# Memory numerators and denominators in one product, and the whole order made anew, in a two-layer Infini-attention and GEGLU block

## The chip, the cores and the metric

One core of one Trainium2 chip runs the whole program in one launch. The metric is the device time in microseconds of one execution. Three runs of the kernel before stand beside a profile of one execution. The core has TensorE (PE in the profile; its weight loads are PEld), VectorE (DVE), ScalarE (ACT), GpSimd (POOL) and SyncE (SP, which here issues nearly all DMAs).

## The reference

The input x has 2048 tokens of 512 values. The program computes attention, then a feed-forward part, and then both again with the same weights. Cut to what matters:

```python
def _A_ref(x, wq, wk, wv, wo, beta):          # H = 32 heads of Dh = 16, N = 4 segments of L = 512
    ...
    for s in range(N):
        logits = einsum('bhqd,bhkd->bhqk', qs, ks) * scale + mask
        a_dot = einsum('bhqk,bhkd->bhqd', softmax(logits), vs)
        pq = phi(qs)                          # phi(t) = t + 1 for t > 0, exp(t) otherwise
        num = einsum('bhld,bhde->bhle', pq, M)
        den = einsum('bhld,bhd->bhl', pq, z)[..., None] + 1e-06
        o = g * (num / den) + (1.0 - g) * a_dot          # g = sigmoid(beta), one value a head
        pk = phi(ks)
        M = M + einsum('bhld,bhle->bhde', pk, vs)        # a 16 x 16 memory for each head
        z = z + einsum('bhld->bhd', pk)                  # and its normaliser, 16 values
    return o @ wo
def _B_ref(x, w_gate, w_up, w_down):          # 512 -> 1792 -> 512
    return _gelu(x @ w_gate) * (x @ w_up) @ w_down
x = x + _A_ref(_layernorm(x), ...); x = x + _B_ref(_layernorm(x), ...)    # and both lines once more
```

## The kernel before, in words

The work is cut into eight blocks k = 0..7: four segments of 512 tokens in the first layer, then the same four in the second. Block k has an attention part (`Att`) and a feed-forward part (`Ffn`). Everything stays in on-chip memory (SBUF) but the weights' first load and the output. Products go to the eight banks of PSUM, 512 float32 values wide; VectorE or ScalarE reads them out from there.

**Attention of one block.** Four tiles `xn` of normalised tokens are transposed to `xnT`, by DMA (line 754, on SP's queue) or by four TensorE transposes against `ident` (line 545). From `xnT` come q, k and v (`wq_sb`, `wk_sb`, `wv_sb`; 12 products of four accumulated matmuls). The scores are made in rounds: 36 rounds a block, taken two at a time, four matmuls side by side on TensorE's four row groups; each pair of rounds fills two pairs of banks, and ScalarE takes the exponential of each pair into `pt` (line 1864). GpSimd masks `pt` (lines 1813 and 1818), and a flush (`flush_item`) multiplies `pt` with v (`vaug`, `vz`) on the four column groups. VectorE turns, divides and turns back the result (lines 1391 to 1414) into `aT`, which meets `wo_sb`.

**Memory.** From block 1 of a layer on, `mem_items` reads the memory: 16 small products of 8 columns give the denominators (`zcols`, line 1195 and the reciprocal in line 1200 make `rdm`), then for each of four groups of 8 heads four products of 128 columns give the numerators (`mblk`), which VectorE scales to `am` (line 1226); a DMA transposes `am` to `amT`, and VectorE adds it to `aT` (line 1417). `upd_item` brings the memory up to date: `spread` writes `mblk` (line 1286) and `z` writes `zcols` (line 1292).

**Feed-forward.** `wo` products are added to `x_sb`, the row statistics are taken (line 856), `xn` is made (line 920) and transposed, then 14 gates, 14 ups and 4 downs per block (four matmuls each, a down has 14) with the gelu on ScalarE.

**What sets the order.** All engines' instructions are recorded in an order that `order()` settles as the program is built. It keeps a clock for each engine (`Clocks`, `Engine`), with fixed costs, picks the item with the earliest due time among those that its clock calls ready (`pick`, `open_item`), and issues scores when ScalarE's queue runs short (`rounds_now`). Some forty numbers (`POLICY`, and `STAGES` for each stretch of 20 us) weigh these choices. Where the clock finds scores still to come but nothing ready, it issues a fill, a product of `warm` that nobody reads. Products go out `whole` (one matmul of 128 x 128 weights) or in `columns` (four matmuls of 32 columns of weights each), whichever stands next to a flush; scores are `rows`. On the chip the engines then follow this order, waiting on each other's semaphores.

Of the kernel before, what the change touches and what calls it, by code (L numbers as in the profile page):

```python
# [17 lines left out]
P = 128  # L18
D = 512
# [13 lines left out]
SCALE = DH ** -0.5  # L33
EPS_LN = 1e-5
# [31 lines left out]
def table(halved):  # L66
# [17 lines left out]
    if halved:  # L84
# [31 lines left out]
    rs_pool=32.757, f_urge=-233.244, quick=2, paired=8, turn_pe=1, turn_last=0, w_at=29.345, w_gap=2.17,  # L116
    wd_at=78.552, wd_gap=2.776, flush_wait=-13.887, piece_slack=40.254, kb_slack=24.368, mem_slack=-20.134,
    margin=0.5, qk_due=0.962, e_q=49.408, e_k=2.993, exp_slack=-6.401, e_slack=131.01, phi_slack=22.785,
    gelu_slack=-0.789, act_evict=1.671, first_evict=0.248, gate_step=93.832, up_due=-100.529, up_step=84.355,
    down_due=-29.196, down_step=-47.297, upd_due=91.807, kb_act=82.777, vz_slack=55.93, x_dve=2.467, v0_due=-11.641,  # L120
    x1_at=-87.497, x2_at=16.051, x3_at=24.107, x3_load=-378.834, direct=2, gelu_tiles=0, look=3, lag=0.852,
    wv_at=-320.502, xn_pool=19.822, kb_pool=121.576, cut_pool=154.009, at_pool=-238.466, pe_turns=0, gate_due=4.191,
    shun=8.799, col_gap=0.807, hold=5, early=104.615, starve=0.16, near=114.234, cap=13, soon=28.208, columns=0,
    kd_slack=-5.85, zero_slack=-1.031, hold1=-49.923, hold2=2.205, hold3=11.541, hold_step=-162.485, hold_v=23.995,
    park=3)

STAGES = [
    (1, 2, dict(
        rs_pool=0.722, quick=9, kb_slack=2.193, mem_slack=-24.231, e_q=-2.643, gelu_slack=-0.49, gate_step=79.021,
        up_due=-101.483, up_step=41.973, down_step=-58.4, upd_due=91.729, vz_slack=33.291, direct=8, gelu_tiles=2,  # L130
        lag=0.412, at_pool=-237.424, early=83.209, starve=60.426, soon=7.146, park=4)),
    (2, 3, dict(
        rs_pool=2.667, quick=6, turn_pe=0, kb_slack=55.298, mem_slack=-32.756, e_q=-2.851, gelu_slack=-0.49,
        gate_step=78.038, up_due=-98.977, up_step=25.491, down_step=-53.827, upd_due=91.729, vz_slack=14.093,
        x_dve=7.459, direct=6, gelu_tiles=2, look=2.764, lag=0.475, xn_pool=30.206, cut_pool=102.189,
        at_pool=-237.424, gate_due=8.415, starve=1.292, soon=7.146, park=5)),
    (3, 4, dict(
        rs_pool=4.794, turn_pe=12, kb_slack=51.509, mem_slack=58.674, e_q=50.036, e_k=1.445, gelu_slack=1.935,
        gate_step=78.038, up_due=-96.513, up_step=85.14, down_step=-56.495, vz_slack=40.138, x_dve=6.187, direct=6,
        look=2.618, xn_pool=30.206, cut_pool=118.125, at_pool=-208.534, gate_due=14.291, shun=21.0, early=101.394,  # L140
        starve=0.321, soon=7.146, park=2)),
    (4, 5, dict(
        rs_pool=-2.341, quick=0, turn_pe=12, kb_slack=85.554, mem_slack=58.674, qk_due=1.009, e_q=50.137, e_k=1.464,
        gelu_slack=0.429, gate_step=79.294, up_due=-96.513, up_step=84.505, down_step=-72.139, vz_slack=51.333,
        x_dve=6.187, direct=3, gelu_tiles=2, xn_pool=20.238, cut_pool=148.746, at_pool=-208.534, gate_due=8.415,
        shun=21.0, early=101.394, starve=0.453, soon=7.146, park=2)),
    (5, 6, dict(
        rs_pool=36.794, quick=0, turn_pe=12, kb_slack=66.017, mem_slack=58.674, qk_due=1.009, e_q=55.15, e_k=2.984,
        gelu_slack=-0.805, gate_step=79.294, up_due=-96.513, down_step=-70.89, vz_slack=18.865, x_dve=7.455,
        gelu_tiles=2, look=2.835, lag=0.71, xn_pool=20.238, cut_pool=148.746, at_pool=-208.534, gate_due=0.276,  # L150
        shun=21.488, soon=7.146)),
    (6, 7, dict(
        rs_pool=11.417, f_urge=-261.392, quick=0, paired=11, turn_pe=0, flush_wait=0.581, piece_slack=36.524,
        kb_slack=76.591, mem_slack=-10.427, qk_due=-0.609, e_q=97.288, e_k=-5.757, exp_slack=-18.942, e_slack=69.536,
        phi_slack=30.587, gelu_slack=0.965, act_evict=1.166, gate_step=33.55, up_due=-80.509, down_due=-55.61,
        down_step=-81.567, upd_due=143.06, kb_act=60.08, vz_slack=4.039, x_dve=18.331, direct=0, gelu_tiles=2,
        look=2.622, lag=0.754, xn_pool=-3.088, kb_pool=116.679, cut_pool=153.155, at_pool=-189.709, gate_due=0.226,
        shun=85.539, hold=8, early=169.131, starve=0.31, near=101.522, cap=11, soon=0.694, kd_slack=37.99, park=6)),
    (7, 8, dict(
        rs_pool=-52.581, f_urge=-61.761, quick=3, paired=0, turn_pe=13, flush_wait=-3.039, piece_slack=92.516,  # L160
        kb_slack=220.906, mem_slack=57.517, qk_due=-30.647, e_q=-54.782, e_k=89.983, exp_slack=-17.861,
        e_slack=55.594, phi_slack=96.482, gelu_slack=214.751, act_evict=-149.173, gate_step=5.34, up_due=-0.69,
        up_step=3.923, down_due=12.354, down_step=-3.42, upd_due=-3.412, kb_act=75.691, vz_slack=-199.522,
        x_dve=3.843, direct=4, gelu_tiles=6, look=1.342, lag=0.004, xn_pool=-28.912, kb_pool=53.965, cut_pool=27.06,
        at_pool=-56.962, gate_due=-1.429, shun=104.852, hold=14, early=6.432, starve=57.777, near=-2.631, cap=0,
        soon=-55.855, kd_slack=-7.989, park=5)),
    (8, 9, dict(
        rs_pool=-52.581, f_urge=-145.617, quick=3, paired=0, turn_pe=9, flush_wait=-5.724, piece_slack=95.692,
        kb_slack=220.647, mem_slack=59.145, qk_due=-29.873, e_q=-54.782, e_k=89.76, exp_slack=-17.752,
        e_slack=55.641, phi_slack=95.445, gelu_slack=218.63, act_evict=-149.173, gate_step=5.34, up_due=-2.89,  # L170
        up_step=10.443, down_due=12.354, down_step=-3.42, upd_due=-3.412, kb_act=75.691, vz_slack=-188.382,
        x_dve=3.864, direct=5, gelu_tiles=6, lag=0.004, xn_pool=-26.431, kb_pool=53.965, cut_pool=27.06,
        at_pool=-56.962, gate_due=-1.429, shun=104.852, hold=14, early=6.432, starve=57.777, near=-2.631, cap=0,
        soon=-86.977, kd_slack=-7.989, park=5)),
    (9, 10, dict(
        rs_pool=-12.084, f_urge=-80.924, paired=7, turn_pe=0, flush_wait=-10.54, piece_slack=101.497,
        kb_slack=138.651, mem_slack=41.847, qk_due=-0.927, e_q=5.553, e_k=3.345, exp_slack=8.894, e_slack=112.615,
        phi_slack=35.259, gelu_slack=68.681, act_evict=-22.963, gate_step=1.861, up_due=1.655, up_step=-0.829,
        down_due=2.632, down_step=52.765, upd_due=23.459, kb_act=0.175, vz_slack=70.28, x_dve=6.676, direct=3,
        look=3.63, lag=0.192, xn_pool=166.767, kb_pool=117.564, cut_pool=-34.878, at_pool=-118.909, gate_due=-0.418,  # L180
        shun=0.067, hold=0, early=-9.041, starve=0.14, near=123.977, cap=10, soon=-75.197, kd_slack=-0.85, park=4)),
    (10, 11, dict(
        rs_pool=14.701, f_urge=-84.002, quick=4, paired=3, turn_pe=0, flush_wait=1.591, piece_slack=2.503,
        kb_slack=15.492, mem_slack=-87.956, qk_due=-1.255, e_q=-12.885, e_k=30.907, exp_slack=-49.037,
        e_slack=61.889, phi_slack=62.891, gelu_slack=12.108, act_evict=-26.178, gate_step=1.032, up_due=-0.726,
        up_step=0.248, down_due=2.892, down_step=13.594, upd_due=48.393, kb_act=-2.244, vz_slack=6.293,
        x_dve=-53.841, direct=7, gelu_tiles=4, look=0.488, lag=0.594, xn_pool=9.388, kb_pool=94.753, cut_pool=-5.876,
        at_pool=-15.364, gate_due=2.814, shun=1.865, hold=4, early=0.773, starve=0.337, near=15.239, cap=8,
        soon=11.166, kd_slack=-1.019, park=4)),
    (11, 12, dict(  # L190
        rs_pool=18.476, f_urge=-83.81, quick=3, paired=2, turn_pe=2, flush_wait=1.611, piece_slack=1.938,
        kb_slack=15.492, mem_slack=-82.753, qk_due=-1.255, e_q=13.513, e_k=-8.54, exp_slack=-36.188, e_slack=75.196,
        phi_slack=62.891, gelu_slack=10.942, act_evict=-15.505, gate_step=0.996, up_due=-0.689, up_step=0.248,
        down_due=6.859, down_step=13.594, upd_due=46.726, kb_act=4.652, vz_slack=6.293, x_dve=-55.157, direct=6,
# [378 lines left out]
def order(pol, nc, cst, seg, wrk, psp, A_x, A_wq, A_wk, A_wv, A_wo, A_beta, B_x, B_w_gate, B_w_up, B_w_down, out):  # L573
# [185 lines left out]
    class Psum:  # L759
# [6 lines left out]
        def read(self, t):  # L766
            banks[self.bank] = t + 0.05
# [1239 lines left out]
```

## Time and profile before

| what | before |
|---|---|
| three runs | 534.12, 535.46, 538.31 us; median 535.46 |
| span of the profiled execution | 533.3 us; its own device time isn't listed apart, and the three runs lie 0.9 to 5.1 us over its span |
| busy: PE, PEld, DVE, ACT, POOL | 524.7, 275.7, 434.6, 445.8, 252.5 us |
| granted TensorE clock | 1.000 over the whole span |
| fetches of instructions by DMA | 83 of 16 KB on one queue, 21 smaller ones on another |

The span runs from the first instruction to the last. The device time of a run lies around it and is a few microseconds longer. A matmul's row gives a duration with its latency, and matmuls overlap; what TensorE spends on one is read from the distance of two starts.

### The profile page before, as it was taken

What the parts mean: (1) busy time and instruction counts of PE and PEld (TensorE: products, weight loads), DVE (VectorE), ACT (ScalarE), POOL (GpSimd) and SP (SyncE); (2) the same over time, 40 slices, a digit from 0 to 9 for tenths busy, and PEclk for the clock granted to TensorE, in tenths of its full rate; (3) what the DMA queues carried; (4) which work ended last, traced back from release to release, by engine and by line L of the source; (5) the groups of instructions that cost most, each with busy time, mean ns of one, the idle gap of its engine ahead of it and who ended that gap; (6) DMA issues with size and microseconds to landing.
All of it is one profiled execution on the core that took longest, in us unless ns stands there. A gap on an engine that the chain in (4) does not pass through costs nothing.

```text
span 533.3 us, 24180 instructions
## 1 busy us (share of the span) xinstructions
PE 524.7 (98%) x10697; PEld 275.7 (52%) x10697; DVE 434.6 (81%) x836; ACT 445.8 (84%) x598; POOL 252.5 (47%) x320
## 2 busy tenths in 40 slices
PE   9999989999999999999999999999999999999997
PEld 4454455444545455555564454555555456555544
DVE  7899997999997999889987788888976997586342
ACT  6999989888999989899898899799979988952320
POOL 2987472548541966428773366391632254400000
PEclk9999999999999999999999999999999999999999
DMA  8367750333330232101221122410250132102101
GB/s 271 76 120 148 190 158 4 69 39 77 42 69 16 53 56 38 32 12 25 53 41 31 25 32 27 60 33 2 53 102 3 33 51 53 23 2 48 37 2 41
DMA packets 76762, 29.99 MB, mean 56 GB/s; under 512 B 61042, under 2 KB 76658, under 8 KB 76658
## 3 DMA queue, kind: packets, MB, share of 16 engines
q1 hardware_dynamic: 76368, 28.20, 25.8%
q8 instruction: 83, 1.36, 1.0%
q10 hardware_dynamic: 290, 0.26, 0.1%
q14 instruction: 21, 0.17, 0.1%
HBM read 9.70 MB, written 2.10 MB: 22 GB/s over the span
## 4 chain that ended last, share of the span: by engine, by line
PE 75%; DVE 5%; ACT 3%; POOL 1%; issue 1%; DMA 1%; ACTq 0%
PE ps L541 75%; ACT pt L1864 1%; DVE xn L920 1%; DVE st L856 1%; ACT gel_sb L1616 1%; POOL kx L726 1%; DVE x_sb L1463 1%; ACT gel_sb L1519 1%; POOL e L1170 1%; DMA xnT<-xn 1%; ACT gel_sb L779 0%; DVE ab L1407 0%; DVE byq L1391 0%; DVE aT L1414 0%; DVE x_sb L869 0%
## 5 line engine op out<-in xcount | busy, mean ns | idle before, releaser
L1864 ACT ACTIVATE pt<-ps 128x1024 bf16<-128x1024 f32 x288 | 279.0, 1036 | 27.5 <-PE ps L541 18.6
L1813 POOL TENSOR_SCALAR_AFFINE_SELECT pt<-pt 128x256 bf16<-128x256 bf16 (+1 forms) x192 | 112.4, 598 | 176.4 <-ACT pt L1864 173.9
L541 PE MATMUL ps<-xnT,wg_sb 128*32 128x512 bf16 (+3 forms) x1367 | 107.7, 362 | 0.2 <-DMA xnT<-xn 0.2
L541 PE MATMUL ps<-wd_sb,gel_sb 128*32 128x512 bf16 (+2 forms) x1431 | 106.1, 354 | 0.0
L541 PE MATMUL ps<-xnT,wu_sb 128*32 128x512 bf16 (+1 forms) x1252 | 103.5, 379 | 0.2 <-ACT gel_sb L1519 0.2
L1557 DVE TENSOR_TENSOR gel_sb<-gel_sb,ps 128x512 bf16<-128x512 bf16 x112 | 75.2, 684 | 30.2 <-PE ps L541 27.9
L541 PEld LDWEIGHTS <-gel_sb 128*32 128x32 bf16 (+1 forms) x1623 | 53.0, 97 | 41.4 <-issue 2.2
L541 PEld LDWEIGHTS <-wu_sb 128*32 128x32 bf16 (+1 forms) x1252 | 45.6, 97 | 45.4 <-issue 2.1
L541 PEld LDWEIGHTS <-wg_sb 128*32 128x32 bf16 (+1 forms) x1367 | 47.4, 97 | 38.7 <-issue 1.4
L1391 DVE STREAM_TRANSPOSE byq<-ps 128x512 f32<-128x512 f32 x64 | 45.3, 709 | 24.0 <-PE ps L541 23.3
L1170 POOL TENSOR_SCALAR e<-e 128x512 bf16<-128x512 bf16 x32 | 49.5, 1550 | 7.0 <-ACT e L1147 6.4
L1463 DVE TENSOR_TENSOR x_sb<-x_sb,ps 128x512 bf16<-128x512 bf16 (+1 forms) x54 | 34.1, 636 | 17.9 <-PE ps L541 17.8
L1818 POOL TENSOR_SCALAR_AFFINE_SELECT pt<-pt 64x1024 bf16<-64x1024 bf16 x32 | 38.5, 1203 | 20.7 <-ACT pt L1864 17.4
L541 PE MATMUL ps<-xnT,wk_sb 128*32 128x512 bf16 (+2 forms) x330 | 34.8, 377 | 0.7 <-ACT pt L1864 0.7
L541 PE MATMUL ps<-pt,vaug 128*32 128x256 bf16 (+2 forms) x1344 | 35.1, 239 | 0.1
L541 PE MATMUL ps<-xnT,wq_sb 128*32 128x512 bf16 (+2 forms) x339 | 34.0, 377 | 0.0
L1616 ACT ACTIVATE gel_sb<-gel_sb 128x1024 bf16<-128x1024 bf16 (+4 forms) x31 | 33.3, 1157 | 0.0
L541 PE MATMUL ps<-wv_sb,xnT 128*32 128x512 bf16 (+1 forms) x227 | 32.4, 380 | 0.8 <-DVE x_sb L1463 0.4
L541 PE MATMUL ps<-q,kx 32*128 32x64 bf16 (+2 forms) x1120 | 31.6, 217 | 0.6 <-ACT pt L1864 0.3
L541 PEld LDWEIGHTS <-vaug 128*32 128x32 bf16 x1344 | 27.1, 97 | 9.2 <-issue 1.6
L856 DVE BATCH_NORM_STATS2 st<-x_sb 128x6 f32<-128x512 bf16 x46 | 31.3, 680 | 0.4
L541 PEld LDWEIGHTS <-kx 32*128 32x128 bf16 x1120 | 17.0, 92 | 28.2 <-issue 27.4
(127 smaller groups left out, 708.7 us busy)
## 6 DMA issues: line engine op xcount, KB each, us to landing
vz<-vaug SPq DMA_DIRECT2D x14, 136.0 KB, 2.9
wg_sb<-in_B_w_gate_dram SPq DMA_DIRECT2D x8, 224.0 KB, 2.9
wu_sb<-in_B_w_up_dram SPq DMA_DIRECT2D x8, 224.0 KB, 3.9
wd_sb<-in_B_w_down_dram SPq DMA_DIRECT2D x7, 256.0 KB, 5.9
x_sb<-in_A_x_dram SPq DMA_DIRECT2D x3, 512.0 KB, 6.7
out_dram<-x_sb SPq DMA_DIRECT2D x12, 128.0 KB, 1.9
xnT<-xn SPq DMA_TRANSPOSE x56, 2.6
kx<-kf SPq DMA_DIRECT2D x12, 64.0 KB, 3.2
```

What stands on the lines that cost most here:

```text
L541: self.nc.tensor.matmul(*args, **kw)
L726: return lambda: eng.tensor_scalar(out=kx[:, :, C * which:C * which + n], in0=kf[:, :, 0:n], scalar1=masks[:, which:which + 1], scalar2=No ...
L856: nc.vector.bn_stats(out=self.st6[:, 0, :], in_=x_sb[:, self.tt0 + j, :])
L920: eng.tensor_scalar(out=xn[:], in0=x_sb[:, self.tt0 + j, :], scalar1=self.mv[:, j, 1:2] if self.wide else self.mv[:, j, 0:1], scalar2=self ...
L1170: lambda eng: eng.tensor_scalar(out=e[0][:], in0=e[0][:], scalar1=1.0, scalar2=None, op0=ALU.min), summed)
L1391: nc.vector.transpose(out=(self.byq[:, pars[0], :, :].rearrange("p a c -> p (a c)") if h is None else self.byq[:].rearrange("p u a c -> p ...
L1463: ck.dve.post(ck.made(), slack, (0.15 + 0.00104 * (c1 - c0), lambda: nc.vector.tensor_tensor(out=xt, in0=xt, in1=ps()[:, 0:c1 - c0], op=AL ...
L1557: ck.dve.post(ck.made(), NORMAL, (0.683, lambda: nc.vector.tensor_tensor(out=g, in0=g, in1=ps()[:], op=ALU.mult), lambda t: (ps.read(t), e ...
L1616: return (0.205 + 0.427 * (f1 - f0), lambda: nc.scalar.activation(out=g, in_=g, func=ACT.Gelu_apprx_tanh), lambda t: self.gelu_done(t, f0, ...
L1813: nc.gpsimd.affine_select(out=view, in_=view, pattern=[[0, 4], [0, n], [1, C]], compare_op=ALU.is_ge, fill=0.0, base=C, channel_multiplier=-1)
L1818: nc.gpsimd.affine_select(out=view, in_=view, pattern=[[0, 4 * TPS], [1, C]], compare_op=ALU.is_ge, fill=0.0, base=0, channel_multiplier=-1)
L1864: nc.scalar.activation(out=pt_all[:, s0:s0 + 2, 2 * p:2 * p + 2, :].rearrange("p r h c -> p h r c"), in_=ps_all[:, pair[0]:pair[1] + 1, :] ...
```

## The change

- **Memory read.** Denominators become a ninth part of the numerators: `mz` holds for each head 16 columns of M and one of z, so 136 columns a group of 8 heads instead of 128 and 8 apart. Instead of 16 products of 8 columns and then 16 of 128 there are 16 of 136. They come in three items; each fills a pair of neighbouring banks (`Pair`), two items with one and a half groups and one with one. VectorE then does, for each item in one go, the denominators, a reciprocal and the scaling.
- **Memory update.** `spread` writes `mz` in four instructions instead of one.
- **Scores.** Where enough banks are free, the four banks of two rounds are taken by one exponential of 2048 columns instead of two of 1024 (`joined`).
- **Head.** The product for beta uses all 128 rows (`beta_row` is cleared by GpSimd first) and stands one product later. GpSimd clears the two `kx` tiles instead of VectorE, and writes the constant columns of three of four v tiles.
- **End.** The last down product of each block of the second layer is cut 384 + 128 instead of 256 + 256.
- **Planner's clock.** Each fetch of TensorE's instructions now makes a busy stretch on SP's queue: an SP instruction that ends near it ends later, and a DMA transpose that starts near it lands later, and no sooner than 0.45 us after the one before. All numbers of `POLICY` and `STAGES` are new, and with them the order of all engines.

```diff
+MZ = (DH + 1) * 8
 POLICY = dict(
-    rs_pool=32.757, f_urge=-233.244, quick=2, paired=8, turn_pe=1, turn_last=0, w_at=29.345, w_gap=2.17,
+    rs_pool=-104.717, f_urge=-138.301, quick=0, paired=6, turn_pe=0, turn_last=0, w_at=29.345, w_gap=-0.624,
...
     # Engine.serve, for SP
+            for begin, end in self.fetches[-3:]:
+                if -0.15 < begin - t < (0.85 if cost > 1.0 else 0.35):
+                    t = max(t, end + (0.45 if begin > t else 1.07) - cost)
     # Clocks.issue
             self.asked.append(self.pe)
+            begin = self.pe + 1.1
+            self.fetches.append((begin, begin + (1.5 if self.dma > begin else 1.05)))
     # Clocks.landing
-        for a in self.asked[-3:]:
-            if -0.6 < a + 1.1 - t < 1.1:
-                got = max(got, a + 2.3 + (1.5 if a + 1.1 < t + 0.1 else 1.1))
+        for begin, end in self.fetches[-3:]:
+            if -0.5 < begin - t < 1.3:
+                got = max(got, end + (1.55 if begin < t + 0.3 else 1.1))
+        self.turned = got = max(got, self.turned + 0.45)
     # head
-    nc.scalar.dma_start(out=beta_row[:], in_=A_beta.partition_broadcast(1))
+    nc.scalar.dma_start(out=beta_row[0:1, :], in_=A_beta.partition_broadcast(1))
+    for kx in kxs:
+        nc.gpsimd.memset(kx.bitcast(mybir.dt.uint32)[:, :, :, C // 2:3 * C // 2], 0)
-    te.matmul(beta_ps, lhsT=warm[0:1, :], rhs=beta_row[:], start=True, stop=True)
     a0.first_q(ps2, 0, half)
+    te.matmul(beta_ps, lhsT=warm[:], rhs=beta_row[:], start=True, stop=True)
     # mem_items
-                product(dens()[:, j, b, :], self.phiq[:, b, j * P:(j + 1) * P], mem_state[k - 1][1][:, b, :])
-                    product(ps()[:, j * P:(j + 1) * P], self.phiq[:, b, j * P:(j + 1) * P], mem_state[k - 1][0][:, b, :])
+            parts = [((0, 0, None), (1, 4, 0)), ((2, 0, None), (1, 4, 1)), ((3, 0, None),)]
+                ps = Pair()
+                    product(ps()[:, i, MZ * u:MZ * u + MZ], self.phiq[:, b, j * P:(j + 1) * P], mem_state[k - 1][0][:, b, :])
+                    steps = [(0.175, den(whole, 0, 2, 0, 4), None)]
+                    if half:
+                        steps.append((0.157, den(1, 2, 3, 4, 6), None))
+                    steps.append((0.454 if half else 0.354, inverse, None))
+                    if half:
+                        steps.append((0.42, scale(1, 2, 3, 4, 6, 2 * n, 2 * n + 2), None))
+                    steps.append((0.69, scale(whole, 0, 2, 0, 4, 0, TPS), told))
+                    ck.dve.post(ready, NORMAL, *steps)
     # Ffn, second layer
-                downs[-1:] = [down(TPS - 1, 0, D // 2), down(TPS - 1, D // 2, D)]
+                downs[-1:] = [down(TPS - 1, 0, D - P), down(TPS - 1, D - P, D)]
     # score
+        joined = bool(runs) and len(got) - 4 >= pol.join
...
+            def exp_all(b0=pairs[0][0]):
+                nc.scalar.activation(
+                    out=pt_all[:, s0:s0 + 2, :, :].rearrange("p r h c -> p h r c"),
+                    in_=ps_all[:, b0:b0 + 4, :].rearrange("p h (r c) -> p h r c", r=2), func=ACT.Exp, scale=SCALE)
```

**VectorE at the first memory read** (block 1; `gel_sb` are the feed-forward's products, `ab`, `aT` the attention's, `e` and `zk` the keys' phi). Before:

```order
L1195 SCALAR_TENSOR_TENSOR rdm<-ps,tmp_e_135 128x128
L1200 RECIPROCAL rdm<-rdm 128x128
L1557 TENSOR_TENSOR gel_sb<-gel_sb,ps 128x512 x3
L1226 TENSOR_TENSOR am<-ps,rdm 128x512 x2
L1557 TENSOR_TENSOR gel_sb<-gel_sb,ps 128x512 x3
```

Now:

```order
L1227 SCALAR_TENSOR_TENSOR rdm<-ps,tmp_e_138 128x32
L1227 SCALAR_TENSOR_TENSOR rdm<-ps,tmp_e_138 128x16
L1235 RECIPROCAL rdm<-rdm 128x48
L1242 TENSOR_TENSOR am<-ps,rdm 128x256
L1242 TENSOR_TENSOR am<-ps,rdm 128x512
L1227 SCALAR_TENSOR_TENSOR rdm<-ps,tmp_e_138 128x32
```

Before, the feed-forward's multiplications stand between the steps of the memory read; now five instructions stand together for each of the first two items, and the two items follow each other.

**SyncE's queue near the end** (`xnT<-xn` is the transpose for a normalised tile, `amT<-am` that of the memory's part, `out_dram` the output). Before:

```order
L754 DMA_TRANSPOSE amT<-am 128x4x128 x2
L600 DMA out_dram<-x_sb 128x256 x2
L754 DMA_TRANSPOSE amT<-am 128x4x128 x2
L754 DMA_TRANSPOSE xnT<-xn 128x4x128 x4
L600 DMA out_dram<-x_sb 128x512 x3
```

Now:

```order
L752 DMA_TRANSPOSE xnT<-xn 128x4x128 x4
L599 DMA out_dram<-x_sb 128x512
L599 DMA out_dram<-x_sb 128x384
L599 DMA out_dram<-x_sb 128x128
L752 DMA_TRANSPOSE amT<-am 128x4x128 x4
L599 DMA out_dram<-x_sb 128x512 x3
```

The four transposes for the last block's feed-forward are gone from the queue; TensorE makes them (16 transposes of 128 x 128 between the downs of block 6). Over the whole program SP issues 40 instead of 56 transposes of `xn`, and TensorE 96 instead of 32.

More of the change, by code (lines that the diff above doesn't have):

```diff
@@ L152 @@
-    (6, 7, dict(
[L153 to L158, printed above, removed]
@@ L159 @@
-    (7, 8, dict(
[L160 to L166, printed above, removed]
```

544 lines of the change are left out of this document (298 added, 246 removed).

## The prediction

> **What bounds the kernel now.** I read the page's busy times and the chain that ended last, then busy times by stretch, then TensorE's own order of time at the holes.
>
> ```profile
> span 533.3 us, 24180 instructions
> PE 524.7 (98%) x10697; PEld 275.7 (52%) x10697; DVE 434.6 (81%) x836; ACT 445.8 (84%) x598; POOL 252.5 (47%) x320
> PE 75%; DVE 5%; ACT 3%; POOL 1%; issue 1%; DMA 1%; ACTq 0%
> ```
>
> TensorE is busy for 98% of the span and holds three quarters of the chain. So only two things move the time: how much TensorE has to do, and how long it stands still. The stretches (columns: width, then busy time of PE, PEld, DVE, ACT, POOL, granted clock, DMA share and rate) show where it stands.
>
> ```profile
> 0.00:9.00 9.00, 7.77 (x43) 3.79 (x44) 5.82 (x19) 5.32 (x13) 2.16 (x14) 1.00 0.80 241
> 20.00:40.00 20.00, 19.68 (x386) 10.09 (x388) 17.66 (x38) 19.89 (x31) 17.34 (x23) 1.00 0.54 107
> 40.00:60.00 20.00, 19.28 (x486) 10.26 (x475) 17.84 (x34) 19.92 (x25) 13.39 (x19) 1.00 0.75 165
> 60.00:80.00 20.00, 18.28 (x361) 9.70 (x359) 18.56 (x39) 17.42 (x30) 12.04 (x13) 1.00 0.59 165
> 80.00:100.00 20.00, 19.78 (x364) 10.04 (x366) 15.37 (x27) 19.50 (x24) 3.84 (x7) 1.00 0.12 29
> 120.00:140.00 20.00, 19.30 (x460) 9.66 (x453) 19.10 (x40) 18.06 (x27) 14.83 (x18) 1.00 0.38 65
> 140.00:160.00 20.00, 19.55 (x336) 9.88 (x338) 19.29 (x35) 19.18 (x26) 8.91 (x12) 1.00 0.32 61
> 180.00:300.00 120.00, 119.77 (x2401) 64.11 (x2400) 106.10 (x201) 108.24 (x140) 69.69 (x83) 1.00 0.20 38
> ```
>
> Of the 8.6 us of idle time (533.3 - 524.7), 1.2 lie in the first 9 us, and 4.1 between 20 and 160: 0.32, 0.72, 1.72, 0.22, 0.70 and 0.45. The 120 us after 180 lose 0.23. ScalarE or VectorE is full in the losing stretches (19.9 of 20 at 20 to 60, 19.1 and 19.3 at 120 to 160). The granted clock, third from the end of each row, is 1.00 everywhere, so throttling plays no part.
>
> ```profile
> 70.15 0.55 PE L541 MATMUL ps<-warm 128*128 128x128 bf16 x7
> ...
> 71.12 0.20 PE L541 MATMUL ps<-q,kx 32*128 32x64 bf16 x1
> 71.58 0.29 PE L541 MATMUL ps<-q,kx 32*128 32x64 bf16 x7 [0.26 <-ACT pt L1864]
> ...
> 74.56 0.29 PE L541 MATMUL ps<-q,kf 16*128 16x64 bf16 x7
> 76.09 0.36 PE L541 MATMUL ps<-q,kf 16*128 16x192 bf16 x5 [1.24 <-issue]
> q8 instruction: 83, 1.36, 1.0%
> ```
>
> Seven fills in a row at 70.15 mark a place with nothing to do. The largest hole, before 76.09, is put down to no engine, in a place with short matmuls and many instructions; I take it for a late fetch of instructions (queue q8, 83 of them). Note what idle leaves out: from 71.12 to 71.58 pass 0.46 us, while matmuls side by side start within a few ns, yet only 0.26 count as idle, because the latency of the one before covers the rest. So a hole costs about 0.17 to 0.2 more than it shows. With some twenty holes (my estimate), the 4.1 us are about 8.
>
> **The change, part by part.** First, what a product costs. The distance between starts, not the duration, is TensorE's price.
>
> ```profile
> 97.18 2.76 PE L541 MATMUL ps<-xnT,wu_sb 128*128 128x512 bf16 x12
> 99.87 0.41 PE L541 MATMUL ps<-q,kx 32*128 32x64 bf16 x20
> 100.21 0.40 PE L541 MATMUL ps<-mblk,phiq 128*128 128x128 bf16 x4
> 100.44 1.03 PE L541 MATMUL ps<-xnT,wu_sb 128*128 128x512 bf16 x4
> 101.31 0.39 PE L541 MATMUL ps<-mblk,phiq 128*128 128x128 bf16 x4
> ...
> 387.80 1.91 PE L541 MATMUL ps<-wd_sb,gel_sb 128*32 128x512 bf16 x32
> 389.64 0.40 PE L541 MATMUL ps<-q,kf 16*128 16x256 bf16 x12
> ```
>
> Four products of 512 columns take 101.31 - 100.44 = 0.87, 0.217 each; four of 128 take 0.23, 0.057 each. From 97.18 to 99.87, twelve of 512 (2.60) leave 0.09 for the change from whole array to row groups. In column groups eight products (32 matmuls) and such a change take 1.84: 8 x 0.217 + 0.10. So a product costs the same in either form, and a change of form 0.1.
>
> ```profile
> L541 PE MATMUL ps<-zcols,phiq x192: 166/166/179, 89.8 to 439.3; 128*32 128x8 bf16 x128, 128*128 128x8 bf16 x64
> L541 PE MATMUL ps<-zcols,phiq x64: 166/174/178, 89.8 to 90.3; 128*32 128x8 bf16 x64
> L541 PE MATMUL ps<-mblk,phiq 128*128 128x128 bf16 x67 | 5.9, 219 | 0.2 <-ACT pt L1864 0.2
> L541 PE MATMUL ps<-mblk,phiq 128*32 128x128 bf16 x116 | 3.0, 219 | 0.0
> L545 PE MATMUL ps<-ident,xn 128*128 128x128 bf16 x32 | 2.9, 220 | 0.1
> L541 PE MATMUL ps<-warm 128*128 128x128 bf16 x11 | 1.1, 218 | 0.0
> L541 PE MATMUL ps<-warm 128*32 128x128 bf16 x8 | 0.5, 219 | 0.0
> ```
>
> - **Memory read: -2.4.** Six reads have 96 denominators (64 whole, 128 / 4 in columns) and 96 numerators. At 89.8 sixteen denominators take 0.5, 0.03 each: 2.9 go, and with them 96 x 0.057 = 5.5. In their place come 96 of 136 columns, 0.057 x 136 / 128 = 0.061 each: 5.9. The sum is -2.5 by these rows; I take -2.4.
> - **Transposes: +3.6.** TensorE makes 96 instead of 32: 64 x 0.057. Their cover was the DMA, which charged TensorE nothing. The Trainium skill, "VectorE: DVE Perf Modes", section "The three transpose paths", gives 390 ns for one on TensorE and 1309 by DMA, and by that, as an estimate, 64 would cost 25 us and the sum would be 21 higher. The row of 32 speaks against it as a price of TensorE's time: 2.9 us in all, at most 0.09 each.
> - **Fills: -0.7.** In the new order one of 13 (11 and 8 / 4) is left: 12 x 0.057.
> - **Changes of form: +1.2.** Counted over all TensorE rows of both orders there are 292 before and 304 now: 12 x 0.1. Also, fewer products are in columns, so TensorE has 18,384 rows instead of 21,396, and the 83 fetches become about 71.
> - **Head and end: -0.3.** Below nothing for the end: the last addition is 0.42 for 256 columns, now 128, so between 0 and 0.42 goes; I take 0.13 by proportion. The one-row product for beta caused two changes of form on the way in and out, about 0.17. GpSimd's clearing falls in its idle time at the start, and frees VectorE in 9 to 20.
>
> ```profile
> 530.41 0.42 DVE L1463 TENSOR_TENSOR x_sb<-x_sb,ps 128x256 bf16<-128x256 bf16 x1 [1.11 <-PE ps L541]
> L1195 DVE SCALAR_TENSOR_TENSOR rdm<-ps,tmp_e 128x128 f32<-128x128 f32 x6 | 1.7, 278 | 0.0
> L1200 DVE RECIPROCAL rdm<-rdm 128x128 f32<-128x128 f32 x6 | 5.7, 953 | 0.2
> L1401 DVE RECIPROCAL r<-byq 128x32 f32<-128x32 f32 x32 | 11.3, 354 | 1.1
> L1226 DVE TENSOR_TENSOR am<-ps,rdm 128x512 bf16<-128x512 f32 x24 | 15.9, 678 | 1.0 <-PE ps L541 1.0
> ```
>
> - **VectorE: +7, off the path.** A read took 0.28 + 0.95 + 4 x 0.68 = 3.95. Now a full item has two short sums (about 0.2 each), a reciprocal of 48 (0.354 + 16 x 0.6 / 96 = 0.45), a scaling of 256 (0.42 by the addition above) and one of 512: 1.95; the last item 1.23. Together 5.1, so 1.2 more a read, 7 in all, on an engine that is 81% busy. Its cover is the feed-forward's products; without it each read would show 1.2.
> - **The holes: -4.0, the choice on which the sum hangs.** The bounds are 8 (all go) and, below nothing, 8 of new ones. For a gain: the fills tell where TensorE had nothing ready, and 12 of 13 go; the 1.72 at 60 to 80 lie there, with hidden time some 2.5; the thinner instruction stream makes a late fetch rarer; exponentials of all four banks and VectorE's freed start ease 20 to 60. Against all of it: what waits for ScalarE at 20 to 60 stays, and the new order has its own tight places. I take half.
>
> **The sum:** -2.4 + 3.6 - 0.7 + 1.2 - 0.3 = +1.4, and -4.0 for the holes: -2.6. The span goes from 533.3 to 530.7. The median of the runs, 535.46, is 2.2 over the span, which the change doesn't touch, so 532.9.
>
> **The rivals.** *Holes only move* (chance 0.24): the work of TensorE is what is left, +1.4: 536.9. For it: the end has become tight. Before, the last gates had room:
>
> ```profile
> 481.77 12.29 PE L541 MATMUL ps<-wd_sb,gel_sb 128*32 128x512 bf16 x280
> 485.94 5.91 SPq L754 DMA_TRANSPOSE xnT<-xn  x4
> 493.89 2.33 PE L541 MATMUL ps<-xnT,wg_sb 128*32 128x512 bf16 x40
> ```
>
> From the end of the `wo` products (481.77) to the first gate pass 12.1 us of downs, and the transposes have landed or nearly by 491.9, 2 us early. In the new order 14 products each of 512, 384 and 128 columns and 16 transposes stand there (3.0 + 2.3 + 0.8 + 0.9 = 7.0 us), while the additions, statistics and normalisation alone ran to about 486.9, 5.1 us; a late step on VectorE would show at once.
>
> *All holes go* (0.17): 8 instead of 4: 528.9. Against it: ScalarE's 19.9 of 20.
>
> *Memory reads starve the scores* (0.11), the side on which the change is slower. Each of 18 items holds two neighbouring banks until VectorE has done all its steps, up to 1.95 instead of 0.68 for one bank: 18 x 1.27 = 23 us more of holding. If VectorE comes late, a pair of rounds finds no two free pairs, ScalarE runs dry, and TensorE has nothing to follow. It decides where VectorE is over 95% (the stretches from 120 to 160); if half of the 23 reach TensorE, 11 on top of 532.9: about 544. Against it: most reads lie after 180, where VectorE has 12% free.
>
> *A transpose costs TensorE 0.39*, the mechanism to which the page's figure belongs: by the busy 0.09 a transpose it is all but shut out (0.01, about 554).
>
> **How the numbers follow.** The forecast has 0.47. The range of 528.5 to 539 takes in it, the two rivals on either side of it and the scatter of the runs (534.1 to 538.3), and leaves out the starved scores. One per cent, 5.4 us, is about what a measurement of this kernel tells from no change: faster means under 530.1, slower over 540.8. Faster has the 0.17 of all holes gone and 0.03 of the forecast's edge, 0.20; slower 0.12; same 0.68.
>
> **What would show it.** In the profile after: TensorE's idle time in 20 to 160 near 2 instead of 4.1, no gap of over 1 us at issue near 75, fetches near 71, `mz` products 0.06 apart, transposes 0.057 apart. Wrong would be: waits of the exponentials for VectorE around `am`, gaps before the last block's gates or `wo` products, or idle time after 180 above 1 us.

## The result and the profile after

| | before | now |
|---|---|---|
| median of four runs each | 535.33 us (534.12 to 538.31) | 557.30 us (555.29 to 557.96) |
| ratio | | 1.040, 95% interval 1.037 to 1.043 |
| profiled execution: span, TensorE idle | 533.3, 8.6 us | 553.4, 30.9 us |

The prediction was 532.9, with 528.5 to 539.0. The change costs 22 us by the medians and 20.1 by the two profiled spans, and the profile shows most of it as idle time of TensorE. The page's head and its chain:

```profile
span 553.4 us, 21067 instructions
...
PE 522.5 (94%) x9116; PEld 265.5 (48%) x9191; DVE 442.6 (80%) x892; ACT 444.0 (80%) x576; POOL 259.1 (47%) x341
...
q8 instruction: 72, 1.18, 0.9%
...
PE 64%; DVE 12%; ACT 10%; DMA 5%; issue 5%; POOL 3%; SPq 0%; DVEq 0%; ACTq 0%; POOLq 0%
```

By these rows TensorE's busy time has gone down by 2 and its idle time up by 22, and its share of the chain from 75% to 64%. Some 6 us of the idle time are not real: 9116 matmuls stand beside 9191 weight loads, so 75 records are missing. In the three runs further below that keep TensorE's order and have all records it is busy for 529 to 531 us, so the idle time has grown by about 16. The stretches, for the same times as before:

```profile
20.00:40.00 20.00, 18.59 (x396) 9.20 (x397) 19.02 (x39) 19.35 (x28) 16.57 (x23) 1.00 0.82 145
...
180.00:300.00 120.00, 113.09 (x2086) 56.98 (x2094) 98.39 (x196) 97.61 (x118) 58.37 (x72) 1.00 0.16 29
300.00:420.00 120.00, 113.14 (x2113) 58.88 (x2125) 94.24 (x193) 100.40 (x136) 57.98 (x75) 1.00 0.12 25
```

The last of these rows before:

```profile
300.00:420.00 120.00, 119.90 (x2641) 63.45 (x2640) 99.67 (x188) 109.43 (x143) 56.62 (x70) 1.00 0.24 41
```

Before, the 120 us after 180 lost 0.23 and the next 120 us 0.10; now each loses 6.9, of which 1.4 and 1.3 are missing records. On average no engine is full there (DVE 98 and 94 of 120, ACT 98 and 100), and the clock is 1.00, so too much work on another engine does not explain the idle time. The waits say for what TensorE stood still (columns: total, times, longest):

```profile
PE ps L539 <- DMA xnT<-xn: 6.4, 8, 1.5
PE ps L539 <- issue: 6.2, 39, 0.2
PE ps L539 <- POOL pt L1865: 5.1, 5, 1.5
PE ps L539 <- ACT pt L1917: 2.9, 9, 1.0
PE ps L539 <- DVE gel_sb L1600: 1.9, 6, 0.6
```

Before, there was none for POOL or `gel_sb` of VectorE, and these two rows were:

```profile
PE ps L541 <- ACT pt L1864: 1.5, 5, 0.4
PE ps L541 <- DMA xnT<-xn: 0.2, 1, 0.2
```

The 39 gaps of 0.2 at "issue" are the missing records and not waits: in the three runs with the same order and all records this row is gone. The timeline at one of the five POOL waits shows the pattern:

```profile
358.07 2.04 ACT L1917 ACTIVATE pt<-ps 128x1024 bf16<-128x1024 f32 x2
...
360.17 2.43 POOL L1865 TENSOR_SCALAR_AFFINE_SELECT pt<-pt 64x1024 bf16<-64x1024 bf16 x2 [1.99 <-ACT pt L1917]
...
360.49 0.63 PE L539 MATMUL ps<-pt,vaug 128*32 128x256 bf16 x24
...
362.65 0.30 PE L539 MATMUL ps<-pt,vz 128*32 128x64 bf16 x16 [1.53 <-POOL pt L1865]
```

The flush starts at 360.49, though the last mask that it needs ends at 362.60; TensorE issues its first 24 matmuls and then stands still with the rest at the head of its queue. GpSimd is not late: it started as soon as the exponentials were done. **The flush was put too early in the order.** Two lines of the program, unchanged by the diff, can do that:

```python
for ck.back in (pol.lag, 0.0):       # a flush is ready if each mask's end + 0.1 + ck.back <= ck.pe
t3 = ck.landing(t2) + margin         # when a DMA transpose counts as landed
```

`lag` and `margin` are safety margins in us. In before `lag` is 0.004 to 1.414 and `margin` 0.5 in all 27 stretches of 20 us. In the new set `lag` is -7.9 to -56.6 in 21 of them, and `margin` -0.5 to -66.6 in all. In the other six, up to 60 us and from 100 to 160, `lag` is 7.7 to 37.9, and none of the five mask waits lies there: they come between 199 and 451 us. Below zero, an input counts as there before its end; far below zero, as soon as its end is merely known. The order's clock does not charge the wait, so it sees neither a hole nor the need for a fill.

### The profile page after: what moved, and what is told of

It is laid out like the page before. It is cut to its first block, busy times and chain, and to the rows that moved or that the text cites. A ratio compares the mean times of both kernels' runs of the same rounds, so it can differ in the third digit from the quotient of the medians.

```text
span 553.4 us, 21067 instructions
## 1 busy us (share of the span) xinstructions
PE 522.5 (94%) x9116; PEld 265.5 (48%) x9191; DVE 442.6 (80%) x892; ACT 444.0 (80%) x576; POOL 259.1 (47%) x341
## 4 chain that ended last, share of the span: by engine, by line
PE 64%; DVE 12%; ACT 10%; DMA 5%; issue 5%; POOL 3%; SPq 0%; DVEq 0%; ACTq 0%; POOLq 0%
PE ps L539 63%; ACT pt L1917 7%; DMA xnT<-xn 5%; DVE gel_sb L1600 2%; POOL pt L1865 1%; DVE x_sb L1506 1%; DVE byq L1434 1%; DVE st L861 1%; DVE xn L925 1%; PE ps L543 1%; ACT gel_sb L1562 1%; ACT gel_sb L1659 1%; DVE ab L1450 1%; DVE pt L1870 1%; DVE aT L1457 1%
## 5 line engine op out<-in xcount | busy, mean ns | idle before, releaser
L1917 ACT ACTIVATE pt<-ps 128x1024 bf16<-128x1024 f32 x264 | 252.7, 1038 | 34.6 <-PE ps L539 30.4
L539 PE MATMUL ps<-xnT,wg_sb 128*32 128x512 bf16 (+1 forms) x745 | 105.5, 380 | 4.8 <-DMA xnT<-xn 1.4
L539 PE MATMUL ps<-wd_sb,gel_sb 128*32 128x512 bf16 (+4 forms) x1177 | 102.0, 368 | 3.3 <-issue 1.7
L539 PEld LDWEIGHTS <-gel_sb 128*32 128x32 bf16 (+1 forms) x1383 | 50.5, 97 | 46.6 <-DVE gel_sb L1600 2.0
L539 PEld LDWEIGHTS <-wg_sb 128*32 128x32 bf16 (+1 forms) x766 | 42.5, 97 | 47.9 <-issue 3.7
L1175 POOL TENSOR_SCALAR e<-e 128x512 bf16<-128x512 bf16 x34 | 54.2, 1605 | 13.3 <-ACT e L1152 11.4
L1506 DVE TENSOR_TENSOR x_sb<-x_sb,ps 128x512 bf16<-128x512 bf16 (+2 forms) x58 | 36.6, 641 | 19.2 <-PE ps L539 18.4
L1865 POOL TENSOR_SCALAR_AFFINE_SELECT pt<-pt 64x1024 bf16<-64x1024 bf16 x24 | 28.5, 1189 | 28.9 <-ACT pt L1917 26.7
L861 DVE BATCH_NORM_STATS2 st<-x_sb 128x6 f32<-128x512 bf16 x50 | 33.8, 676 | 0.2
L539 PE MATMUL ps<-wo_sb,aT 128*32 128x512 bf16 (+1 forms) x283 | 31.2, 380 | 1.0 <-ACT pt L1917 0.5
```

The source lines that it names most:

```text
L539: self.nc.tensor.matmul(*args, **kw)
L861: nc.vector.bn_stats(out=self.st6[:, 0, :], in_=x_sb[:, self.tt0 + j, :])
L1175: lambda eng: eng.tensor_scalar(out=e[0][:], in0=e[0][:], scalar1=1.0, scalar2=None, op0=ALU.min), summed)
L1506: ck.dve.post(ck.made(), slack, (0.15 + 0.00104 * (c1 - c0), lambda: nc.vector.tensor_tensor(out=xt, in0=xt, in1=ps()[:, 0:c1 - c0], op=AL ...
L1865: nc.gpsimd.affine_select(out=view, in_=view, pattern=[[0, 4 * TPS], [1, C]], compare_op=ALU.is_ge, fill=0.0, base=0, channel_multiplier=-1)
L1917: nc.scalar.activation(out=pt_all[:, s0:s0 + 2, 2 * p:2 * p + 2, :].rearrange("p r h c -> p h r c"), in_=ps_all[:, pair[0]:pair[1] + 1, :] ...
```

## Experiments

**Theories.** A: these two numbers put products ahead of their inputs. B: the new parts (memory read in pairs of banks, joined exponentials, more TensorE transposes) make the waits. C: any order made anew misses the chip, since the old one fits it.

All results side by side. The first seven experiments after "now" are one run each, the others medians of 4 to 12. Idle is the span less TensorE's busy time. Fills are products of `warm` 128 wide (whole ones, and columns by four). "DMA" and "masks" are TensorE's waits for transposes by DMA and for `pt` by GpSimd. Five rows have idle time that is 5 to 7 us too high for missing records: now, `lag` -30, `lag` alone held up, new last down, and half masks on VectorE.

| kernel | time | idle | DMA | masks | fills |
|---|---|---|---|---|---|
| before | 535.3 | 8.6 | 0.2 | 0 | 13 |
| now | 557.3 | 30.9 | 6.4 | 5.1 | 1 |
| old code, `margin` -5 | 551.4 | 20.2 | 7.9 | 0 | 17 |
| old code, `lag` -30 | 588.6 | 44.5 | 5.2 | 10.0 | 111 |
| new code, `lag` and `margin` held up | 568.3 | 23.5 | 0 | 0.2 | 108 |
| new code, `lag` alone held up | 579.7 | 35.3 | 3.7 | 0 | 131 |
| old code, all new numbers | 603.6 | 46.7 | 4.9 | 13.0 | 104 |
| new code, all old numbers | 576.5 | 32.2 | 11.5 | 0.6 | 143 |
| old code, new last down | 549.9 | 25.1 | 6.1 | 0 | 25 |
| now, half masks on VectorE | 557.7 | 31.7 | 6.6 | 0.4 | 1 |
| now, half masks out | 554.5 | 18.9 | 8.2 | 0.3 | 1 |
| now, transposes of a weight | 547.4 | 15.9 | 0 | 5.0 | 1 |
| now, both | 542.0 | 11.0 | 0 | 0.3 | 1 |
| new code, numbers anew | 536.8 | 10.3 | 0 | 0 | 12 |
| the same, second set | 537.8 | 9.7 | 0 | 0 | 13 |

In each of the seven the whole order is made anew, and a set of numbers that wasn't chosen for it packs badly. This shows as fills and a long time. The granted clock of these runs was lower too: 0.977 with the old code and all new numbers, 0.985 to 0.988 in the three that took 576 to 589 us, 0.994 to 0.997 in the others. So what tells the theories apart there is the kind of wait, not the time.

### Each number alone in the old code

```diff
-    ...pol.margin...                       # at all five places
+    ...-5.0...
```

> Before with one number changed: each DMA transpose counts as landed 5 us sooner than the order's clock has it (margin -5 instead of 0.5 and 0) the whole way; lag stays between 0.0 and 1.4. Theory A: only the waits for a DMA's xnT (and phik, amT) appear, 5 to 9 us where before had 0.2; the waits for pt by GpSimd stay at 0 to 0.5; time 539 to 546. Rival B: no new part is in, so 535 to 538 and under 1 us of such waits. Rival C: waits of every kind, pt by GpSimd and ScalarE among them, 545 or more.

```profile
PE ps L541 <- DMA xnT<-xn: 6.9, 7, 1.9
PE ps L541 <- ACT pt L1864: 2.5, 6, 0.8
```

With 1.0 more for `phik` the DMA waits are 7.9, and there is no wait for a mask: as A has it. The time is 5 us above A's range. TensorE also waits more for ScalarE (2.5 for `pt` and 1.4 for `gel_sb`, before 1.5 and 0.2), and the one run of before beside it took 538.1; both count for a part of that.

```diff
-            for ck.back in (pol.lag, 0.0):
+            for ck.back in (-30.0, 0.0):
```

> Before with only lag set to -30 throughout; margin stays 0.5 or 0; the order is made anew. Theory A: waits for pt, behind GpSimd's masks and behind exponentials of ScalarE, appear, 10 us or more together where before had 1.5; waits for a DMA's xnT stay under 1.5; the order is also packed worse, 575 to 590 us. Rival B: no such waits, 555 to 562.

```profile
PE ps L541 <- POOL pt L1818: 8.5, 6, 1.9
...
PE ps L541 <- DMA xnT<-xn: 4.4, 3, 2.2
PE ps L541 <- ACT pt L1864: 3.9, 9, 0.7
```

With 1.5 more for GpSimd's other masks and the 3.9 for exponentials, `pt` comes late by 13.9 us (and by 2.3 more for masks on VectorE) in a code without any new part: B is out as the sole cause of such waits. The DMA row is a miss of A's expectation (4.4 instead of under 1.5). Its longest wait, 2.2, is before the last block's gates, where no scores are left, so the order fills no hole; the cause of the other two stays open.

### Held up in the new code

```diff
-            for ck.back in (pol.lag, 0.0):
+            for ck.back in (max(pol.lag, 0.0), 0.0):
-    ...pol.margin...
+    ...max(pol.margin, 0.5)...
```

> After with the two numbers held up: lag no lower than 0, margin no lower than 0.5; everything else as in after, the order made anew. Theory A: the waits for xnT by DMA and pt by GpSimd fall from 11.5 us to under 2; what the order's clock had left out now shows as fills, 50 to 150 of them instead of 1, and since the other numbers were not chosen for this the time is 555 to 570. Rival B: joined exponentials, pairs and transposes are all still there, so 8 us or more of those waits stay. Rival C: as B, and for all engines.

No wait for a transpose by DMA is left, and for masks 0.2:

```profile
PE ps L539 <- ACT pt L1917: 5.3, 16, 0.5
PE ps L539 <- ACT gel_sb L1562: 3.4, 2, 2.0
...
PE ps L539 <- POOL pt L1865: 0.2, 1, 0.2
```

Pairs, joined exponentials and TensorE's transposes are all still there. I read the 108 fills as what the negative numbers had hidden. The time is 11 us longer than now: held up, these other numbers don't pack the work.

> After with only lag held up to 0 or more; margin stays negative; the order is made anew. Theory A, each number has its own wait: the waits for pt (GpSimd's masks) fall from 5.1 us to under 1; waits for a DMA's xnT stay, 3 to 6 us, because the margin still counts the transposes as landed too soon; fills in place of the rest, 565 to 575 us. Rival B (new parts): both kinds stay.

(the first of the two edits alone). No mask of GpSimd is waited for, and 3.0 us for `xnT` and 0.7 for `phik` stay, as A has it. But TensorE waits 10.0 us for ScalarE's `pt`, 2.9 in now, and the time, 579.7, lies above the range; the granted clock was 0.988 in this run.

### Code and numbers exchanged

> The code of before, built with all numbers of after (join and col_pool, which it doesn't know, left out); the order is made anew. Two of the numbers say when an input counts as there: lag (0.0 to 1.4 us of margin before, down to -56 in after) and margin, which is added to a DMA transpose's landing (0.5 or 0 before, down to -66 in after). Theory A, the negative numbers put products ahead of their inputs and the order's clock does not charge the wait: TensorE's waits for xnT by DMA and for pt by GpSimd, 11.5 us together in after and 0.2 in before, are 8 us or more here, and the time is 575 to 590 (bad packing on top). Rival B, the new parts (memory read in pairs of banks, joined exponentials, more TensorE transposes) make the waits: the old code has none of them, so at most 1 us of such waits, 555 to 565. Rival C, every order made anew misses the chip: waits of all kinds, also for VectorE and ScalarE, grow alike.

> The code of after (memory read in pairs, TensorE's fetches in the order's clock, the new head and end), built with the numbers of before, exponentials never joined; the order is made anew. Theory A: lag and margin are not below zero, so the waits for xnT by DMA and pt by GpSimd fall from 11.5 us to under 2, but the numbers don't suit this code, so the order's clock sees many places with nothing ready: over 100 fills, 560 to 570 us. Rival B (the new code makes the waits): 8 us or more of those waits remain, 570 to 580. Rival C: 8 us or more, of all kinds.

The masks' waits go with the numbers: 13.0 us in the old code with the new set, 0.6 in the new code with the old set. The rest is less clear. In the first run the time, 603.6, is over A's range, and waits for VectorE and ScalarE grew as well, as C has it; in before there were 1.5 for ScalarE's `pt` and none for `am`:

```profile
PE ps L527 <- POOL pt L1804: 9.8, 8, 2.1
PE ps L527 <- ACT pt L1850: 5.7, 14, 0.8
PE ps L527 <- DVE am L1212: 4.5, 5, 2.2
```

The second run took 576.5 us with 12.1 of the two waits, which is what B had forecast, and a clear miss of A: 11.5 for DMA where A said under 2 for both. These are three waits, and one of them is 7.9:

```profile
270.91 11.30 SPq L762 DMA_TRANSPOSE amT<-am  x3
...
276.03 1.20 DVE L935 TENSOR_SCALAR xn<-x_sb,mv,rs 128x512 bf16<-128x512 bf16 x2 [1.69 <-POOL rs L914]
...
280.31 0.69 DVE L1470 TENSOR_TENSOR aT<-aT,amT 128x512 bf16<-128x512 bf16 x1
...
282.26 5.20 SPq L762 DMA_TRANSPOSE xnT<-xn  x4
...
286.10 1.46 PE L549 MATMUL ps<-wv_sb,xnT 128*128 128x512 bf16 x3 [7.91 <-DMA xnT<-xn]
```

The third transpose of `am` was issued only at 281.0, when VectorE's addition had read the old `amT` (280.31 + 0.69); four transposes of `xn` stand behind it in SP's queue, two of which had their `xn` since 277.2. I read that as a hole by queue order and not by the two numbers; no run here undoes it, so against B this run counts for the masks alone. Neither the old nor the new numbers are safe for a code that they weren't chosen for.

### One part of the change alone

```diff
-                downs[-1:] = [down(TPS - 1, 0, D // 2), down(TPS - 1, D // 2, D)]
+                downs[-1:] = [down(TPS - 1, 0, D - P), down(TPS - 1, D - P, D)]
```

> Before with one part of the change alone: the last down of each block of the second layer cut 384 + 128 instead of 256 + 256, all numbers as they were. The order is made anew, though no number changed. Theory A: lag and margin are as before, so no product stands ahead of its input: TensorE's waits for xnT by DMA and pt by GpSimd stay under 1.5 us together; what is lost shows as fills (25 or so instead of 13) and a few us of worse packing, 538 to 546. Rival C (every order made anew misses the chip): 5 us or more of such waits.

```profile
504.23 1.06 PE L541 MATMUL ps<-xnT,wg_sb 128*32 128x256 bf16 x32 [4.04 <-DMA xnT<-xn]
506.84 1.47 PE L541 MATMUL ps<-xnT,wg_sb 128*32 128x256 bf16 x24 [1.55 <-DMA xnT<-xn]
```

No mask is waited for, and 5.6 of the 6.1 us for transposes lie before the last block's gates. Still A's expectation failed twice (under 1.5 us of waits, 538 to 546 us), and C's 5 us or more came: a cut that moves 128 columns from one product to another, with all numbers kept, cost 14.6 us. C has a part: whatever changes a cost makes the order anew, and its worth is then that of an unchosen order. So in this program one part of a change can't be priced by undoing it while the order is made anew.

Taken together, the mask waits follow `lag` in every order: 5.1 to 13.0 us where it is far below zero, 0 to 0.6 where it is not. The transposes don't follow `margin` alone. They are waited for where it is below zero (3.7 to 7.9), but also in three orders where it is not (5.2, 6.1 and 11.5).

### The waits taken away in an unchanged order

In the next four, TensorE's order is that of now, row for row; only what is issued elsewhere differs.

```diff
-            ck.pool.post(..., (Port(1.14), lambda: mask_half(slot, 1), done.append), ...)
+            ck.pool.post(..., (Port(1.14), lambda: mask_dve(slot, 1), done.append), ...)   # the same half, on VectorE
```

> After with TensorE's order unchanged, row for row: of the 12 rounds whose mask GpSimd makes in two halves (1.14 us each, one after the other) the second half is made by VectorE at the same place of the program. In after TensorE waits 5.1 us in 5 places for the second half. Theory A (those flushes stand 1 to 2.4 us ahead of their masks, so the time is lost on the spot and not given back): the waits for GpSimd's half masks fall to under 1.5 us and the run is 3 to 5 us shorter than after's 557.3, 552 to 554.5. Rival B (the flush waits for other things too, or another wait takes the place): within 1.5 us of 557.3. Against a gain: VectorE has 12 instructions of about 0.4 to 0.7 us more.

The mask wait fell to 0.4, and nothing was gained. The twelve halves took VectorE far more than I had put:

```profile
L1871 DVE TENSOR_TENSOR pt<-pt,tri 64x1024 bf16<-64x1024 bf16 x12 | 13.5, 1126 | 0.4
```

TensorE's waits for `gel_sb` by VectorE rose from 1.9 to 3.8, and 1.7 for these masks and 1.1 for `macc` came up. By itself the run would speak for rival B of its expectation, another late input behind each wait; but it added 13.5 us to an engine in the way, for a reason told in the last section. So the work was left out instead:

```diff
-            ... (Port(1.14), lambda: mask_half(slot, 1), done.append) ...
+            ... (Port(1.14), None, done.append) ...
```

> After with TensorE's order unchanged; the second half mask of the 12 rounds that GpSimd masks in two halves is left out (part of the causal mask is missing, so the output differs). Unlike the run with those halves on VectorE this adds no work anywhere. Theory P, a wait is lost on the spot: the 5.1 us of waits for GpSimd's half masks shrink to 1 or less and the time falls by 4 to 5, to 552 to 553.5. Theory Q, the products behind are ahead of their other inputs as well, so the next late input takes the wait over: the wait row shrinks alike, but the time falls by 0 to 2, to 555.3 to 557.3.

```diff
-    turn_later(..., lambda: xn()[:], landed, ...)
+    turn_later(..., lambda: w_att["q"][:, 0, :], landed, ...)
```

> After with TensorE's and VectorE's order unchanged; the 40 DMA transposes for xnT read a weight tile that is always there instead of xn, so that SP need not wait for VectorE before it issues them (the output differs). Theory P: the 6.4 us of waits for a DMA's xnT shrink to 1 to 2 and the time falls by 4 to 6, to 551 to 553.5. Theory Q: the wait row shrinks alike, the time falls by 0 to 3. A third way, in which the transfers themselves and SP's queue set the landing: the row stays at 4 or more and so does the time.

> After with TensorE's order unchanged and both taken away: the 12 second half masks left out, and the 40 DMA transposes reading a weight tile (the output differs). Theory P: the sum of the two, 8 to 11 us, 546 to 549. Theory Q: less than half of it, 552 to 556, with waits for ScalarE's pt and VectorE's gel_sb, 2.9 and 1.9 in after, growing by what the others lose.

The spans and TensorE's busy time of the three, in this order:

```profile
span 549.7 us, 21146 instructions
...
PE 530.8 (97%) x9191; PEld 265.6 (48%) x9191; DVE 441.9 (80%) x892; ACT 443.7 (81%) x576; POOL 244.8 (45%) x329
```

```profile
span 545.5 us, 21073 instructions
...
PE 529.6 (97%) x9191; PEld 265.6 (49%) x9191; DVE 442.1 (81%) x892; ACT 443.1 (81%) x576; POOL 256.8 (47%) x341
```

```profile
span 540.2 us, 21077 instructions
...
PE 529.2 (98%) x9191; PEld 265.3 (49%) x9191; DVE 441.2 (82%) x892; ACT 442.5 (82%) x576; POOL 242.7 (45%) x329
```

Medians: 554.5 (551.6 to 557.2), 547.35 and 542.02, against 557.30. Without the halves 2.8 are gained, between theory P (4 to 5) and Q (0 to 2). Its four runs spread with the granted clock, 551.6 and 552.8 at 1.000, 556.2 and 557.2 at 0.994, and in its profile the waits for `xnT` rose from 6.4 to 8.2, so a part was handed on. Without the wait for `xn` 9.95 are gained, more than the 4 to 6, and without both 15.3, more than the 8 to 11. The profiled spans, of which now's is the shortest of four, fit closer: from 553.4 to 540.2 it is 13.2, against 11.5 us of waits (6.4 + 5.1 in 13 places), each of which is some 0.2 longer than it shows, since the latency of the matmul before covers the rest. With both gone, no other wait took their place but 0.8 more for `xn` and 0.4 for a load of `vz`:

```profile
PE ps L539 <- DVE gel_sb L1600: 1.9, 6, 0.6
PE ps L539 <- ACT pt L1917: 1.8, 7, 0.3
...
PE ps L543 <- DVE xn L925: 1.0, 1, 1.0
```

In now these had 1.9, 2.9 and 0.2. So the expectation's theory P holds for the two together, with its sizes off: a product that is put too early loses its wait on the spot. Two thirds of the 22 us hang on the masks and the transposes that the order counts as there. What is left, 542.0 against 535.3, no run takes apart.

### The new code with numbers chosen anew

The code of the change, with `lag` 0.0 to 1.5 and `margin` 0.5, and all other numbers of `POLICY` and `STAGES` searched on the order's own clock under that limit.

> The code of after, row for row, with another set of numbers: lag between 0.0 and 1.5, margin 0.5, all others chosen anew on the order's own clock under that limit. Theory A (the loss of after lies in the two numbers below zero): TensorE's waits for a DMA's xnT and for GpSimd's pt together under 2.5 us, span 534 to 540, time 536 to 542, at least 15 us below after. Rival B (pairs of banks, joined exponentials and the new clock cost by themselves): waits of 8 us or more and 548 or more.

> As the run before, with a second set of numbers under the same limits (TensorE makes 80 instead of 64 of the transposes of xn, and there are more instructions). Theory A: 537 to 545, waits for a DMA's xnT and GpSimd's pt under 2.5 us together. Rival B: 550 or more, with those waits at 8 us or more.

The ratios to before are 1.0007 (0.9985 to 1.0029) and 1.0028 (1.0005 to 1.0051). The first one's page:

```profile
span 535.5 us, 23035 instructions
...
PE 525.2 (98%) x10133; PEld 271.9 (51%) x10133; DVE 437.0 (82%) x888; ACT 445.9 (83%) x588; POOL 252.1 (47%) x329
```

Its longest waits of TensorE:

```profile
PE ps L613 <- ACT pt L1991: 1.8, 5, 0.5
PE ps L617 <- DVE xn L999: 1.3, 1, 1.3
```

No wait for a transpose by DMA or a mask of GpSimd is among TensorE's. The same code runs 20.5 us faster than now, and as fast as before; an order made anew need not miss the chip, which answers C, and B's waits are gone with all the parts in place. How much a part is used is itself up to the numbers: in the two sets 9 and 23 exponentials are joined (12 in now), and TensorE makes 64 and 80 transposes (96). Under these sets the change neither gains nor costs much (the intervals leave -0.15% to +0.29% and +0.05% to +0.51%): the 22 us came with the numbers. As all numbers were chosen anew, these two runs don't show how much of it is due to `lag` and `margin` alone; for that stand the two thirds above. No set tried here was faster than before.

## Why the prediction was wrong

- **TensorE's work: right.** Priced row by row with the steps that I had read (0.217 for 512 columns, 0.057 for 128, 0.1 a change of form), the order of now comes to 516.7 us against 515.1, +1.6; I had +1.4. The `mz` products start 0.059 apart (0.061 expected), the transposes 0.056 (0.057); 1 fill is left, and there are 72 fetches (71 expected).

```profile
L543 PE MATMUL ps<-ident,xn 128*128 128x128 bf16 x96 | 7.9, 220 | 0.5 <-ACT pt L1917 0.3
L539 PE MATMUL ps<-mz,phiq 128*128 128x136 bf16 x80 | 6.2, 223 | 0.0
L539 PE MATMUL ps<-warm 128*128 128x128 bf16 x1 | 0.2, 219 | 0.0
```

- **The holes, -4.0: the step that failed.** Starts later than those steps allow add up to 14.0 us before and 32.8 now: +18.8. Of these, 7.1 are more waits for transposes, 6.0 for half masks, some 3 for `gel_sb` and some 2 for ScalarE's `pt`. My bounds were 8 either way. I said that "the fills tell where TensorE had nothing ready, and 12 of 13 go". Fills tell where the order's clock sees nothing ready. With `lag` and `margin` below zero it nearly always sees something, so here the fills went, 13 to 1, while TensorE's idle time grew. The diff showed `lag=0.852` beside `lag=-7.912` and `margin=0.5` beside `margin=-4.735`; I read the two sets as opaque and looked at neither.
- **Idle time from 20 to 160, near 2:** the six stretches that I had read lose 6.3, some 2 of it missing records, against 4.1 before: nothing was gained there. **Above 1 after 180**, the sign for being wrong, came true with 18.7 from 180 to 500, of which 3.8 are missing records. The two other signs, waits around `am` and gaps before the last gates, did not come.
- **The gap near 75** of over 1 us is gone, as expected, but it was never more than a twentieth of what came.
- **VectorE, +7 off the path: right in size** (434.6 to 442.6, of which the reads' own rows are 23.3 to 30.1) and in that it is covered: TensorE waits 0.3 for `am`.
- **Rivals.** *Holes only move* had the sign and a fifteenth of the size, and its place (last gates) was not it. *Starved scores* was on the right side, the slower one, but by another wait than those that came; 544 was short too. *A transpose at 0.39* is out: 0.056.

## What to carry to other kernels

- Where an order is made by a planner, read the numbers that have a unit first: with a safety margin below zero, this planner issued work before its inputs existed and did not see the wait. Check whether a planner charges for what it assumes.
- Fewer fills or planned stalls prove nothing about an engine's idle time; only a trace does. Here waits before products whose input was still being made, by an engine that had started on time, were waits of order.
- To price a wait, take its cause away with the engine's order unchanged, and add no work elsewhere; an order made anew hides the effect in 10 us or more of packing.

## Of the hardware, not expected

- A half mask on VectorE (64 partitions), while GpSimd masks the other half, took 1.126 us on average; the mask of all 128 partitions took 0.844 in before:

```profile
L1823 DVE TENSOR_TENSOR pt<-pt,tri 128x1024 bf16<-128x1024 bf16 x16 | 13.5, 844 | 0.1
```

The single instructions show why. Ten of the twelve halves started while a mask of GpSimd still had over 0.15 us to run, and each ended 0.52 to 0.54 us after that mask did: one started at 130.42, GpSimd's mask ended at 131.26, and VectorE's 0.54 later. In before and now, 14 of the 36 masks on VectorE started so, and they too ended 0.52 to 0.54 us after GpSimd's; the 11 that started with GpSimd idle took 0.67 to 0.69. So a mask moved to VectorE beside GpSimd's mask mostly waits for that one to end, and VectorE with it. The Trainium skill, "SBUF — State Buffer", section "Who interferes with whom", says that a VectorE instruction with two SBUF inputs contends with a GpSimd instruction that reads SBUF. These masks agree with that; beside other work of GpSimd VectorE's masks took 0.65 to 1.09 us, which no run here takes apart. GpSimd's half took 1.24 beside VectorE's, against 1.19 in the order of now.

- Around the 7.9 us wait in the new code with old numbers the granted clock, third from the end, fell and came back:

```profile
270.00:280.00 10.00, 6.65 (x162) 4.45 (x160) 7.70 (x16) 9.58 (x12) 6.61 (x10) 0.76 0.14 28
280.00:290.00 10.00, 3.90 (x22) 1.35 (x23) 1.78 (x4) 1.30 (x3) 0.46 (x1) 0.56 0.43 88
290.00:300.00 10.00, 10.00 (x130) 4.41 (x132) 9.21 (x23) 8.54 (x14) 3.21 (x6) 1.00 0.03 7
```

The wait alone did not bring it down: it was at 0.52 from 275 to 278 already, where the wait only begins, and from 270 to 275 TensorE had been busy for 3.6 of 5 us at 1.00. In before and now, with no wait above 1.6 us, it stayed at 1.00 in the profiled executions. But with `lag` alone held up, where the longest wait was 1.5 us, its mean was 0.988, so the longest wait does not decide it.
